# A TensorE-bound attention and gated feed-forward kernel: a new table of lead times, the second batch's query projections at the start, and key projections in pieces of 32 columns

## The chip, the cores and the metric

The kernel runs on 1 core of one Trainium2 chip. The metric is the device time of one execution in microseconds. TensorE's records in a profile are PE (matmuls) and PEld (the weight load that stands ahead of each matmul); DVE is VectorE, ACT is ScalarE, POOL is GpSimd, SP is SyncE, which issues all DMAs here.

## The reference

Four batches, four heads, 1088 positions, 32 values a head. A linear attention is followed by a gated feed-forward with mixing over positions.

```python
# attention, per batch b and head h (r = 8)
phi(x) = outer(S1 @ x, S2 @ x)                  # 64 features a position
kv  = sum_s phi(k)[s] v[s]^T ;  z = sum_s phi(k)[s]
att = phi(q) kv / (phi(q) z + 1e-6)             # -> x [4, 1088, 128]
# feed-forward
h = relu(x @ w_in)                              # [128 -> 1024]
u, v = halves of h                              # 512 each
v_n = (v - mean) / sqrt(var + 1e-6)
v_s = w_spatial @ v_n + b_spatial               # over the 1088 positions
out = (u * v_s) @ w_out                         # [512 -> 128]
```

## The kernel before

**Layout.** Positions are taken in 9 tiles of 128 (`kt`), and, where they are columns, in three pieces `CH` of 424, 332 and 332. Almost all matmuls are float32r in three passes of high and low parts: high times high, high times low, low times high. The bulk is `spatial` (lines 989 and 991 for the high weight, 998 and 1000 for the low one), which for each batch, each of 4 blocks of 128 features (`d`) and each column piece (`c`) adds 9 `kt` into one PSUM bank. `hidden_v` makes the half v of the hidden layer (banks `sd`), its statistics on DVE and its norm; `hidden` makes u (bank `pu`); `gate` multiplies and splits; `out_mm` adds into the banks `po`.

**Batches.** Batch 0's attention (`attention0`) runs first and by itself, with the loads of weights beside it. From then on `main(b)` is written next to `attention(b + 1)`, so that the attention of the next batch runs within the matmuls of this one.

**Two short stretches per attention.** In `keys(b)`, for b = 1 to 3, two blocks of plain float32 matmuls interrupt the float32r ones. The profile shows two passes, each with its weight load, for every float32 matmul that is no transpose. The first stretch, `projections`, projects the three pieces of keys (`project`, line 591) and the first piece of query rows (`query(0, 64)`, line 671). From its banks ACT copies one half (line 596) and DVE builds the key features (line 598). The second stretch, `sums`, adds up kv (`part4`, line 641, 72 matmuls of 33 columns with weights of 32) and projects the other two pieces of query rows. `turned` copies a query projection to SBUF on ACT (tile `abT`, line 658), stores it to DRAM (`abd`, line 772), and `query_features` loads it back spread out (`fa`, `fb`, in the ring `pl` of 6 buffers), to be multiplied on POOL (line 779).

**What sets the order.** Nothing is written in its final order. Each step is given to `op` with its engine, a cost, and what it reads and writes; `schedule` works out a due time for each from the end backwards and then lets each engine take, of the steps that can start about then, the one due first. `LEADS`, a table of some 1,600 numbers (ns), moves the due times of single steps or groups; `Fill` puts small matmuls that nothing reads (line 466) where the plan sees TensorE idle at the start. Engines run the resulting streams in order, and SP's single stream issues every load and store. Where a load's buffer is not free yet, all loads behind it wait.

Of the kernel before, what the change touches and what calls it, by code (L numbers as in the profile page):

```python
# [367 lines left out]
def tile_kernel(ctx: ExitStack, tc: tile.TileContext, kT, qT, vA, sks, idn, msk, wT, w_in, w_out, bsp, out):  # L368
# [218 lines left out]
    def project(ab, xt, at=0):  # L587

        for t in range(3):
            for j in range(2):  # L590
                nc.tensor.matmul(ab_view(ab, at)[64 * j:64 * j + 64, :, t], xt[:, t * P + 64 * j:t * P + 64 * j + 64], sk[:, :NSK], start=True, stop=True)
# [19 lines left out]
    def keys(b, qts=()):  # L611

        xts, vs = [], []
        for g in range(3):
            xt = tl("kt", f"kt{b}{g}", [P, 384])
            load(xt, lambda xt=xt, g=g: xt.ap, kT[b, g], 192, after=AFTER[b])
            v_sb = tl("v", f"v{b}{g}", [P, 3, H * (D + 1)])
            load(v_sb, lambda v_sb=v_sb: v_sb.ap.rearrange("p t c -> p (t c)"), vA[b, g], 198, after=AFTER[b])
            xts.append(xt)
            vs.append(v_sb)  # L620
        kv = bank("sd" if b else "pu", f"kv{b}")

        def part(g, f):
            o = kv[:, :132].rearrange("p (r c) -> p r c", r=2)
            for t in range(3):
                for pr in range(2):
                    for i in range(2):
                        c = 128 * pr + 64 * i
                        nc.tensor.matmul(
                            o[64 * i:64 * i + 64, pr], f[:, t, c:c + 64], vs[g][:, t, 66 * pr:66 * pr + 66],  # L630
                            start=(g == 0 and t == 0 and pr == 0), stop=(g == 2 and t == 2 and pr == 1),
                        )

        def part4(g, f):

            o = kv[:, :68].rearrange("p (r c) -> p r c", r=2)
            for t in range(3):
                for pr in range(2):
                    for j in range(4):
                        c, vc = 128 * pr + 32 * j, 33 * (2 * pr + j // 2)  # L640
                        nc.tensor.matmul(
                            o[32 * j:32 * j + 32, pr, :33], f[:, t, c:c + 32], vs[g][:, t, vc:vc + 33],
                            start=(g == 0 and t == 0 and pr == 0), stop=(g == 2 and t == 2 and pr == 1),
                        )

        if not b:
            for g in range(3):
                f = phi(b, g, xts[g], "k")
                op("PE", 705, f4=True, fn=lambda g=g, f=f: part(g, f), r=[f, vs[g]], w=[kv])
            return kv  # L650

        abTs = []

        def turned(g, ab, o):
            k.part = "q", f"q{b}", f"q{b}.{g}"
            n = TW[g] // 2
            abT = tl("abT", f"abT{b}{g}", [P, 192])
            op("ACT", c_act(n, True), lambda: nc.scalar.copy(out=abT[:, :n], in_=ab[:, o:o + n]), r=[ab], w=[abT])
            abTs.append(abT)
            query_features(b, g, abT, query_fs[-1])  # L660

        abs_ = [bank("sd", f"kab{b}{n}") for n in range(2)]
        at = [(abs_[0], 0), (abs_[0], 192), (abs_[1], 0)]
        qat = [(abs_[1], 192), (kv, 68), (kv, 260)]

        def query(g, m):

            (ab, o), n = qat[g], TW[g] // 2
            for f in range(2):
                for r in range(0, 64, m):  # L670
                    nc.tensor.matmul(ab[64 * f + r:64 * f + r + m, o:o + n], sk[:, r:r + m], qts[g][:, f * n:(f + 1) * n], start=True, stop=True)

        def projections():
            for xt, (ab, o) in zip(xts, at):
                project(ab, xt, o)
            query(0, 64)

        op("PE", 1478, f4=True, fn=projections, r=[*xts, qts[0], (sk, "x")], w=abs_)
        turned(0, *qat[0])
        k.part = "k", f"k{b}"  # L680
        fs = [features(b, g, at[g][0], "k", at[g][1], abTs[:1] if g == 2 else ()) for g in range(3)]

        def sums():
            for g in range(3):
                part4(g, fs[g])
            for g in range(1, 3):
                query(g, 32)

        op("PE", 2070, f4=True, fn=sums, r=[*fs, *vs, *qts[1:], (sk, "x")], w=[kv])
        for g in range(1, 3):  # L690
            turned(g, *qat[g])
        k.part = "k", f"k{b}"
        kvs = tl("ka", f"kvs{b}", [P, 68])
        op("ACT", c_act(68, True), lambda: nc.scalar.copy(out=kvs.ap, in_=kv[:, :68]), r=[kv], w=[kvs])
        return kvs
# [4 lines left out]
    def attention0(st):  # L700

        b = 0
        k.part = "k0", "k0.0"
        kv = keys(b)
        op("DVE", 290, lambda: nc.vector.tensor_tensor(
            out=kd0.ap.rearrange("p r a c -> p (r a) c"), in0=kv[:, :132].rearrange("p (q c) -> p q c", q=4),
            in1=mask[:, 2:].unsqueeze(2).broadcast_to([P, 4, D + 1]), op=ALU.mult,
        ), r=[kv, mask], w=[kd0])
        x_tiles(b, st)
        xh, xl = st["xh"], st["xl"]  # L710
        qts = []
        for g in range(3):
            xt = tl("c", f"qt{b}{g}", [P, 384])
            load(xt, lambda xt=xt, g=g: xt.ap, qT[b, g], 192)
            qts.append(xt)
        k.part = ("q0",)
        qps = [phi(b, g, qts[g], "q") for g in range(3)]
        for g in range(3):
            k.part = "n0", f"n0.{g}"
            tags = ("po", "sp")  # L720
            qp = qps[g]
            qpT = []
            for pr in range(2):
# [36 lines left out]
            op("ACT", c_act(384, True), lambda gs=gs, xp=xp: nc.scalar.copy(out=xh[:, gs], in_=xp[:, :384]), r=[xp], w=[(xh, g)])  # L760
            op("DVE", c_dve(384), lambda gs=gs, xp=xp: nc.vector.tensor_tensor(out=xl[:, gs], in0=xp[:, :384], in1=xh[:, gs].bitcast(F32), op=ALU.subtract), r=[xp, (xh, g)], w=[(xl, g)])
        st["lows"] = [tl("vl", f"vl{b}{d}", [P, NK, P], F32R) for d in range(ND)]
        for g in range(3):
            k.part = "h0", f"h0.{g}"
            hidden_v(b, st, g)
# [391 lines left out]
```

## Time and profile before

| | |
|---|---|
| median of 3 runs | 330.2 us (330.13 to 330.75) |
| profiled execution | 330.07 us, of which the span of its instructions 328.2 us |
| PE busy | 319.7 us, 97% of the span, 2553 matmuls |
| DVE, ACT, POOL busy | 200.8, 151.9, 49.0 us |
| granted TensorE clock | 0.999 over the span |
| DMA | 23.95 MB, 73 GB/s mean, most of it in the first 130 us |

The span runs from the first to the last instruction; the other 1.87 us lie around it. PE is busy in nearly every slice of the page, so time is gained here by less work for TensorE or by fewer of its pauses, and an idle stretch of another engine costs nothing unless TensorE waits for it. Starts of neighbouring matmuls tell its pace better than their durations, which overlap.

### The profile page before, as it was taken

The page shows a single profiled execution, that of the slowest core. Times are in us where ns is not written, and L with a number is a line of the kernel's source. Part 1 is how long each engine was busy: PE and PEld are TensorE (multiplying, and loading weights), DVE is VectorE, ACT ScalarE, POOL GpSimd, SP SyncE. Part 2 cuts the span into 40 slices and gives each one's busy share as a digit, 9 for nine tenths or more (in the row PEclk, how much of TensorE's full clock was granted, in tenths as well). Part 3 has the DMA queues.
Part 4 walks back from the last instruction along what each step waited for, and adds up shares of the span by engine and source line. Part 5 has one row for each costly group of instructions (what it writes and reads, how often), then busy time and mean ns, then how long its engine had stood idle before and what let it go on. Part 6 is the DMA issues. An engine that isn't in the chain of part 4 may idle for free.

```text
span 328.2 us, 6446 instructions
## 1 busy us (share of the span) xinstructions
PE 319.7 (97%) x2553; PEld 305.0 (93%) x2553; DVE 200.8 (61%) x437; ACT 151.9 (46%) x358; POOL 49.0 (15%) x60
## 2 busy tenths in 40 slices
PE   8998999999999899999999999999999999999996
PEld 8987999998999789999999999999999999999995
DVE  4999996457899961468799666379863232231113
ACT  2578947434575452435753554456452142121212
POOL 1000104541610014412000143320000000000000
PEclk9999999999999999999999999999999999999999
DMA  6831369534111245200010334000000010000001
GB/s 214 310 94 50 116 172 312 175 108 147 48 47 44 86 147 177 71 0 7 19 45 15 97 111 138 20 2 0 2 0 1 2 47 23 0 0 2 0 2 68
DMA packets 18960, 23.95 MB, mean 73 GB/s; under 512 B 2546, under 2 KB 18674, under 8 KB 18930
## 3 DMA queue, kind: packets, MB, share of 16 engines
q1 hardware_dynamic: 18930, 23.54, 22.7%
q8 instruction: 20, 0.33, 0.4%
q14 instruction: 10, 0.08, 0.1%
HBM read 20.46 MB, written 3.06 MB: 72 GB/s over the span
## 4 chain that ended last, share of the span: by engine, by line
PE 75%; DVE 9%; DMA 7%; ACT 6%; issue 2%; SPq 0%; ACTq 0%; DVEq 0%
PE sp L989 17%; PE sp L991 15%; PE sp L998 15%; PE sd L439 3%; DMA pl<-in_wT 3%; PE sd L441 3%; PE sd L440 3%; PE pu L439 2%; PE po L440 2%; PE po L439 2%; PE po L441 2%; PE pu L441 2%; PE pu L440 2%; DMA out<-u 2%; PE sp L1000 2%
## 5 line engine op out<-in xcount | busy, mean ns | idle before, releaser
L989 PE MATMUL sp<-wT,vh 128*128 128x332 f32 (+1 forms) x414 | 134.1, 325 | 0.2 <-DVE u L1025 0.2
L991 PE MATMUL sp<-wT,vl 128*128 128x332 f32 (+1 forms) x368 | 118.8, 323 | 0.0
L998 PE MATMUL sp<-wT,vh 128*128 128x332 f32 (+1 forms) x368 | 116.9, 322 | 0.0
L989 PEld LDWEIGHTS sp<-wT,vh 128*128 128x128 f32 x414 | 77.9, 188 | 2.3 <-DVE u L1025 0.8
L991 PEld LDWEIGHTS sp<-wT,vl 128*128 128x128 f32 x368 | 69.2, 188 | 0.3
L998 PEld LDWEIGHTS sp<-wT,vh 128*128 128x128 f32 x368 | 69.1, 188 | 0.1
L1025 DVE TENSOR_TENSOR u<-sp,u 128x332 f32<-128x332 f32 (+1 forms) x40 | 20.5, 516 | 57.4 <-PE sp L1000 41.9
L449 DVE TENSOR_TENSOR g<-u,g 128x332 fp32r<-128x332 f32 (+1 forms) x38 | 23.6, 620 | 17.1 <-PE po L440 10.6
L981 ACT ACTIVATE u<-pu 128x332 f32<-128x332 f32 (+1 forms) x40 | 18.5, 463 | 33.4 <-PE pu L441 22.6
L518 ACT CAST g<-u 128x332 fp32r<-128x332 f32 (+1 forms) x38 | 18.2, 484 | 23.8 <-DVE u L1025 18.2
L843 ACT ACTIVATE vt<-sd 128x512 f32<-128x512 f32 x36 | 21.3, 600 | 15.2 <-PE sd L441 14.4
L845 DVE BATCH_NORM_STATS2 st<-vt 128x6 f32<-128x512 f32 x36 | 24.3, 688 | 5.3 <-ACT vt L843 5.1
L779 POOL TENSOR_TENSOR pl<-pl,pl 128x384 f32<-128x384 f32 (+1 forms) x18 | 18.0, 1005 | 63.6 <-DMA pl<-abd 44.6
L905 ACT CAST vh<-vt 128x384 fp32r<-128x384 f32 x36 | 17.7, 511 | 21.1 <-DVE vt L865 12.4
L823 DVE RECIPROCAL c<-c 128x384 f32<-128x384 f32 (+1 forms) x9 | 21.8, 2417 | 5.1 <-ACT c L821 5.1
L452 POOL TENSOR_TENSOR r<-pl,r 128x384 fp32r<-128x384 f32 (+1 forms) x18 | 18.6, 1037 | 23.5 <-ACT r L518 23.5
L907 DVE TENSOR_TENSOR vl<-vt,vh 128x384 fp32r<-128x384 f32 (+1 forms) x36 | 17.5, 503 | 1.9 <-ACT vh L905 1.7
L439 PE MATMUL pu<-x,wih 128*128 128x332 f32 (+1 forms) x48 | 16.6, 346 | 1.1 <-ACT u L981 0.7
L865 DVE TENSOR_SCALAR vt<-vt,mv,sm 128x512 f32<-128x512 f32 x32 | 16.3, 552 | 0.0
L563 ACT CAST wT<-pl 128x332 fp32r<-128x332 f32 (+1 forms) x27 | 12.9, 496 | 6.8 <-DMA pl<-in_wT 6.6
L441 PE MATMUL pu<-x,wil 128*128 128x332 f32 (+1 forms) x48 | 15.7, 327 | 0.0
L440 PE MATMUL pu<-x,wih 128*128 128x332 f32 (+1 forms) x48 | 15.7, 326 | 0.0
(151 smaller groups left out, 494.1 us busy)
## 6 DMA issues: line engine op xcount, KB each, us to landing
pl<-in_wT SPq DMA_DIRECT2D x18, 166.0 KB
v<-in_vA SPq DMA_DIRECT2D x12, 198.0 KB
kt<-in_kT SPq DMA_DIRECT2D x12, 192.0 KB
pl<-abd SPq DMA_DIRECT2D x12, 192.0 KB
pl<-abd SPq DMA_DIRECT2D x24, 96.0 KB
pl<-in_wT SPq DMA_DIRECT2D x9, 212.0 KB
c<-in_qT SPq DMA_DIRECT2D x9, 192.0 KB
out<-u SPq DMA_DIRECT2D x6, 166.0 KB
```

The source lines that it names most:

```text
L439: nc.tensor.matmul(o, ah, bh, start=start, stop=False)
L440: nc.tensor.matmul(o, ah, bl, start=False, stop=False)
L441: nc.tensor.matmul(o, al, bh, start=False, stop=stop)
L449: return lambda: nc.vector.tensor_tensor(out=o(), in0=a(), in1=bb(), op=ALU.subtract)
L452: return lambda: nc.gpsimd.tensor_tensor(out=o(), in0=a(), in1=bb(), op=ALU.subtract)
L823: op("DVE", 135 + 6.3 * n, lambda x32=x32, n=n: nc.vector.reciprocal(out=x32[:, :n], in_=x32[:, :n]), w=[x32])
L843: op("ACT", c_act(512, True) + 16, lambda pv=pv, t=t: nc.scalar.activation(vt[:, t], pv.ap, AF.Relu), r=[pv], w=[(vt, t)])
L845: op("DVE", 690, lambda stats=stats, t=t: nc.vector.bn_stats(out=stats.ap, in_=vt[:, t]), r=[(vt, t)], w=[stats])
L989: nc.tensor.matmul(sp[:, :cw], vh[:, kt], wTh[:, kt, cs], start=(kt == 0), stop=False)
L991: nc.tensor.matmul(sp[:, :cw], vl[:, kt], wTh[:, kt, cs], start=False, stop=False)
L998: nc.tensor.matmul(sp[:, :cw], vh[:, kt], wTl[:, kt, cs], start=False, stop=False)
L1025: op("DVE", c_dve(cw), lambda: nc.vector.tensor_tensor(out=u.ap, in0=sp[:, :cw], in1=u.ap, op=ALU.mult), r=[sp], w=[u], lead=LEAD[1])
```

## The change

The numbers of `LEADS` are replaced (1,577 entries; most differ). They were found with a plan that also counts TensorE's instructions in blocks of 256; the count itself is not in the kernel, whose `schedule` is as before. Batch 1's query rows are loaded into the `u` ring, projected, copied and stored to DRAM within `attention0` (`early_queries`), ahead of `hidden_v`; their spread-out loads (`expanded`) stay in batch 1's attention. `project` takes its pieces from a parameter: 32 columns in the stretches of batches 1 to 3 (twice the matmuls, as many columns each), 64 in batch 0 as before; batches 2 and 3 also take the first query piece in 32s.

```diff
-LEADS = {'W0': -13000, 'W0.1': 20000, 'W0.3': -5740, ...
+LEADS = {'W0': -5650, 'W0.0': 9780, 'W0.1': -16100, ...
...
-    def project(ab, xt, at=0):
+    def project(ab, xt, at=0, m=64):
         for t in range(3):
-            for j in range(2):
-                nc.tensor.matmul(ab_view(ab, at)[64 * j:64 * j + 64, :, t], xt[:, t * P + 64 * j:t * P + 64 * j + 64], sk[:, :NSK], start=True, stop=True)
+            for j in range(0, P, m):
+                nc.tensor.matmul(ab_view(ab, at)[j:j + m, :, t], xt[:, t * P + j:t * P + j + m], sk[:, :NSK], start=True, stop=True)
...
+        late = b > 1
+        behind = []
         def projections():
             for xt, (ab, o) in zip(xts, at):
-                project(ab, xt, o)
-            query(0, 64)
-        op("PE", 1478, f4=True, fn=projections, r=[*xts, qts[0], (sk, "x")], w=abs_)
-        turned(0, *qat[0])
+                project(ab, xt, o, 32)
+            if late:
+                query(abs_[1], 192, qts[0], 0, 32)
+        op("PE", 1380 if late else 1055, f4=True, fn=projections, r=[*xts, *qts[:late], (sk, "x")], w=abs_)
+        if late:
+            behind = [turned(b, 0, abs_[1], 192)]
+            expanded(b, 0)
...
+        qat = [(kv, 68), (kv, 260)] if late else []
         def sums():
             for g in range(3):
                 part4(g, fs[g])
-            for g in range(1, 3):
-                query(g, 32)
+            for g, (ab, o) in enumerate(qat, 1):
+                query(ab, o, qts[g], g, 32)
-        op("PE", 2070, f4=True, fn=sums, r=[*fs, *vs, *qts[1:], (sk, "x")], w=[kv])
+        op("PE", 2062 if late else 1565, f4=True, fn=sums, r=[*fs, *vs, *qts[1:], (sk, "x")], w=[kv])
...
+    def early_queries():
+        b = 1
+        qts = []
+        for g in range(3):
+            k.part = "q", f"q{b}", f"q{b}.{g}"
+            xt = tl("u", f"qt{b}{g}", [P, 384])
+            load(xt, lambda xt=xt, g=g: xt[:, :TW[g]], qT[b, g, :, :TW[g]], 192)
+            qts.append(xt)
+        for gs in ((0, 1), (2,)):
+            ab = bank("po", f"qab{b}{gs[0]}")
+            op("PE", 326 * len(gs), f4=True, fn=lambda gs=gs, ab=ab: [query(ab, 192 * (g % 2), qts[g], g, 64) for g in gs], r=[*(qts[g] for g in gs), (sk, "x")], w=[ab])
+            for g in gs:
+                turned(b, g, ab, 192 * (g % 2))
...
     def attention(b, st):
+        if b == 1:
+            for g in range(3):
+                expanded(b, g)
+        else:
...
             xt = tl("c", f"qt{b}{g}", [P, 384])
             load(xt, lambda xt=xt, g=g: xt[:, :TW[g]], qT[b, g, :, :TW[g]], 192, after=AFTER[b])
```

Three places show how the streams move. Lines 989, 991, 998 and 1000 are 1011, 1013, 1020 and 1022 in the changed kernel, 671 is 764, 742 is 731, 756 is 745, 658 is 770.

**The start.** TensorE's stream about the first `hidden_v` matmuls of batch 0 (`sd` is their bank, `wih` and `wil` the weights, `sp<-abT,c` transposes of x), before:

```order
L441 MATMUL sd_91<-wih_276,x 128x512
L439 MATMUL sd_129<-wih_276,x 128x512
L440 MATMUL sd_129<-wil_288,x 128x512
L441 MATMUL sd_129<-wih_276,x 128x512
L756 MATMUL sp_301<-abT_125,c_160 128x128 x3
```

and now (`u` holds the early query rows, `po` takes their projection):

```order
L441 MATMUL sd_91<-wih_280,x 128x512
L764 MATMUL po_148<-u_188,sk 64x192 x2
L764 MATMUL po_148<-u_197,sk 64x192 x2
L745 MATMUL sp_308<-abT_121,c_163 128x128 x3
L439 MATMUL sd_126<-wih_280,x 128x512
L440 MATMUL sd_126<-wil_290,x 128x512
L441 MATMUL sd_126<-wih_280,x 128x512
```

Two of the three early pieces now stand there, the third further on, right ahead of the batch's last three hidden blocks and the first `spatial` matmul; 17 fills stand in the stream where 16 did. SP's stream at the same place of the program (`kt<-in_w_in` is the last large load of weights ahead of `wT`, the spatial weight), before:

```order
L446 DMA c_160<-in_qT 128x384
L446 DMA kt<-in_w_in 128x1024
L446 DMA b_64<-in_bsp 83x16
L446 DMA pl_187<-in_wT 128x424
L446 DMA pl_196<-in_wT 128x424
```

and now:

```order
L446 DMA c_163<-in_qT 128x384
L446 DMA kt<-in_w_in 128x1024
L446 DMA u_188<-in_qT 128x384
L446 DMA u_197<-in_qT 128x384
L446 DMA pl_213<-in_wT 128x424
L446 DMA b_64<-in_bsp 83x16
L446 DMA pl_229<-in_wT 128x424
```

Two query loads stand ahead of the first six loads of `wT`; the third stands behind them.

**Batch 1's second stretch.** TensorE's stream where `sums` lies (`kp` the key features, `sd` the bank of kv), before:

```order
L998 MATMUL sp_263<-wT,vh 128x332
L641 MATMUL sd_91<-v,kp_143 32x33 x24
L641 MATMUL sd_91<-v,kp_163 32x33 x24
L641 MATMUL sd_91<-v,kp_148 32x33 x24
L671 MATMUL sd_91<-c_146,sk 32x192 x4
L671 MATMUL sd_91<-c_160,sk 32x160 x4
L989 MATMUL sp_263<-wT,vh 128x332
```

and now:

```order
L1020 MATMUL sp_268<-wT,vh 128x332
L641 MATMUL sd_91<-v,kp_161 32x33 x24
L641 MATMUL sd_91<-v,kp_141 32x33 x24
L641 MATMUL sd_91<-v,kp_144 32x33 x24
L1011 MATMUL sp_268<-wT,vh 128x332
L1022 MATMUL sp_268<-wT,v_93 128x332
```

The query rows are gone from it; batches 2 and 3 keep theirs.

**Between batch 2's two stretches.** TensorE's stream behind the first query piece, before (18 matmuls of 424 columns into `sp` follow the three of `pu`, and then `sums`):

```order
L591 MATMUL sd_91<-sk,kt 64x2x32 x12
L591 MATMUL sd_129<-sk,kt 64x2x32 x6
L671 MATMUL sd_129<-c_160,sk 64x192 x2
L439 MATMUL pu_173<-x,wih_67 128x424
L440 MATMUL pu_173<-x,wih_67 128x424
L441 MATMUL pu_173<-x,wil_71 128x424
L989 MATMUL sp_301<-wT,vh 128x424
```

and now (18 of 332 columns follow the three of `po`, and then `sums`):

```order
L591 MATMUL sd_91<-sk,kt 32x2x32 x24
L591 MATMUL sd_126<-sk,kt 32x2x32 x12
L764 MATMUL sd_126<-c_163,sk 32x192 x4
L439 MATMUL po_148<-g,woh 128x332
L440 MATMUL po_148<-g,woh 128x332
L441 MATMUL po_148<-g,wol 128x332
L1011 MATMUL sp_268<-wT,vh 128x332
```

The 21 matmuls in between are narrower. In batch 3, 72 matmuls of 332 columns lay in between, and 24 do now. ACT's stream there in batch 2, before:

```order
L518 CAST g<-u_735 128x332
L658 COPY abT_125<-sd_129 128x192
L596 COPY ka_63<-sd_91 128x96
L596 COPY ka_69<-sd_91 128x96
L596 COPY ka_63<-sd_129 128x96
```

and now:

```order
L871 ACTIVATE sm_516<-mv_486,eps 128x3
L596 COPY ka_63<-sd_91 128x96
L596 COPY ka_69<-sd_91 128x96
L770 COPY abT_121<-sd_126 128x192
L596 COPY ka_63<-sd_126 128x96
```

The copies for two of the three key features stand ahead of the query's there; in batch 3 they stand behind it, as before.

More of the change, by code (lines that the diff above doesn't have):

```diff
@@ L650, in keys @@
             return kv
[L652 to L660, printed above, removed]
         abs_ = [bank("sd", f"kab{b}{n}") for n in range(2)]
         at = [(abs_[0], 0), (abs_[0], 192), (abs_[1], 0)]
[L664 to L671, printed above, removed]
+        late = b > 1
+        behind = []
         def projections():
             for xt, (ab, o) in zip(xts, at):
-                project(ab, xt, o)
-            query(0, 64)
-        op("PE", 1478, f4=True, fn=projections, r=[*xts, qts[0], (sk, "x")], w=abs_)
-        turned(0, *qat[0])
+                project(ab, xt, o, 32)
[5 more added lines that the diff above has]
+            expanded(b, 0)
         k.part = "k", f"k{b}"
-        fs = [features(b, g, at[g][0], "k", at[g][1], abTs[:1] if g == 2 else ()) for g in range(3)]
+        fs = [features(b, g, at[g][0], "k", at[g][1], behind if g == 2 else ()) for g in range(3)]
+        qat = [(kv, 68), (kv, 260)] if late else []
         def sums():
@@ L685, in sums @@
                 part4(g, fs[g])
-            for g in range(1, 3):
-                query(g, 32)
-        op("PE", 2070, f4=True, fn=sums, r=[*fs, *vs, *qts[1:], (sk, "x")], w=[kv])
-        for g in range(1, 3):
-            turned(g, *qat[g])
+            for g, (ab, o) in enumerate(qat, 1):
+                query(ab, o, qts[g], g, 32)
+        op("PE", 2062 if late else 1565, f4=True, fn=sums, r=[*fs, *vs, *qts[1:], (sk, "x")], w=[kv])
+        for g, (ab, o) in enumerate(qat, 1):
+            turned(b, g, ab, o)
+            expanded(b, g)
         k.part = "k", f"k{b}"
@@ L761, in attention0 @@
             op("DVE", c_dve(384), lambda gs=gs, xp=xp: nc.vector.tensor_tensor(out=xl[:, gs], in0=xp[:, :384], in1=xh[:, gs].bitcast(F32), op=ALU.subtract), r=[xp, (xh, g)], w=[(xl, g)])
+        early_queries()
         st["lows"] = [tl("vl", f"vl{b}{d}", [P, NK, P], F32R) for d in range(ND)]
@@ L765, in attention0, with query, turned, expanded @@
             hidden_v(b, st, g)
-    query_fs = []
-    def query_features(b, g, abT, fs):
+    abds, query_fs = {}, {}
+    def query(ab, o, xt, g, m):
+        n = TW[g] // 2
+        for f in range(2):
+            for r in range(0, 64, m):
+                nc.tensor.matmul(ab[64 * f + r:64 * f + r + m, o:o + n], sk[:, r:r + m], xt[:, f * n:(f + 1) * n], start=True, stop=True)
+    def turned(b, g, ab, o):
+        k.part = "q", f"q{b}", f"q{b}.{g}"
         n = TW[g]
-        abd = tl(None, f"abd{b}{g}", [64, n])
+        abT = tl("abT", f"abT{b}{g}", [P, 192])
+        op("ACT", c_act(n // 2, True), lambda: nc.scalar.copy(out=abT[:, :n // 2], in_=ab[:, o:o + n // 2]), r=[ab], w=[abT])
+        abd = abds[b, g] = tl(None, f"abd{b}{g}", [64, n])
         op("SP", 560, lambda: nc.sync.dma_start(out=abd[:, :].rearrange("r (f c) -> f r c", f=2), in_=abT[:, :n // 2]), r=[abT], w=[abd], kb=n // 4, lag=HBM_LAG[0])
+        return abT
+    def expanded(b, g):
+        k.part = "q", f"q{b}", f"q{b}.{g}"
+        n, abd = TW[g], abds[b, g]
         for pr in range(2):
@@ L779, in query_features @@
             op("POOL", c_pool(n), lambda fa=fa, fb=fb: nc.gpsimd.tensor_tensor(out=fa[:, :n], in0=fa[:, :n], in1=fb[:, :n], op=ALU.mult), r=[fb], w=[fa])
-            fs[g, pr] = fa
+            query_fs[b, g, pr] = fa
+    def early_queries():
+        b = 1
+        qts = []
+        for g in range(3):
+            k.part = "q", f"q{b}", f"q{b}.{g}"
+            xt = tl("u", f"qt{b}{g}", [P, 384])
[6 more added lines that the diff above has]
+                turned(b, g, ab, 192 * (g % 2))
     def attention(b, st):
@@ L786, in attention @@
         qts = []
-        for g in range(3):
-            k.part = "q", f"q{b}", f"q{b}.{g}"
-            xt = tl("c", f"qt{b}{g}", [P, 384])
-            load(xt, lambda xt=xt, g=g: xt[:, :TW[g]], qT[b, g, :, :TW[g]], 192, after=AFTER[b])
-            qts.append(xt)
+        if b == 1:
+            for g in range(3):
+                expanded(b, g)
+        else:
+            for g in range(3):
+                k.part = "q", f"q{b}", f"q{b}.{g}"
+                xt = tl("c", f"qt{b}{g}", [P, 384])
+                load(xt, lambda xt=xt, g=g: xt[:, :TW[g]], qT[b, g, :, :TW[g]], 192, after=AFTER[b])
+                qts.append(xt)
         k.part = "k", f"k{b}"
-        fs = {}
-        query_fs.append(fs)
         kv = keys(b, qts)
@@ L814, in attention @@
             for pr in range(2):
-                f = fs[g, pr]
+                f = query_fs[b, g, pr]
                 fh, fl = tl("r", f"fh{b}{g}{pr}", [P, 384], F32R), tl("r", f"fl{b}{g}{pr}", [P, 384], F32R)
```

2 lines of the change are left out of this document (1 added, 1 removed).

## The prediction

> **What bounds the kernel now.** I read the page's sums first, then TensorE's waits, then the windows, and at last its timeline about each place that the change touches.
>
> ```profile
> PE 319.7 (97%) x2553; PEld 305.0 (93%) x2553; DVE 200.8 (61%) x437; ACT 151.9 (46%) x358; POOL 49.0 (15%) x60
> ...
> q8 instruction: 20, 0.33, 0.4%
> ...
> PE sd L671 <- issue: 1.5, 1, 1.5
> ...
> PE sd L439 <- ACT vt L843: 0.9, 1, 0.9
> PE pu L439 <- ACT u L981: 0.7, 2, 0.4
> ...
> 0.00:32.20 32.20, 29.67 (x294) 26.48 (x295) 26.50 (x72) 20.01 (x46) 1.21 (x8) 1.00 0.52 165
> ...
> 60.00:120.00 60.00, 57.79 (x677) 53.88 (x676) 45.63 (x96) 32.25 (x83) 17.23 (x19) 1.00 0.30 92
> 120.00:180.00 60.00, 59.72 (x383) 57.08 (x382) 38.60 (x80) 28.20 (x65) 12.29 (x14) 1.00 0.17 53
> 180.00:240.00 60.00, 59.71 (x499) 56.70 (x498) 41.97 (x89) 30.70 (x73) 13.09 (x14) 1.00 0.16 51
> 240.00:300.00 60.00, 60.00 (x368) 59.38 (x368) 17.69 (x38) 16.57 (x39) 0.00 (x0) 1.00 0.03 10
> ```
>
> TensorE is the bound: from 32 us on it sits idle for 2.21 us in the window to 120, 0.28 in that to 180, 0.29 in that to 240. The largest piece is 1.5 us, its releaser "issue", which means that nothing the profile shows held it. So three things can move the time: that pause, the work that TensorE does after 32 us, and its other waits, 2.78 - 1.5 = 1.3 us in these windows.
>
> **The pause in batch 2's second stretch.** The timeline of PE at the second stretch of batches 1, 2 and 3, with the counts of matmuls up to their starts and up to the pause:
>
> ```profile
> 67.69 1.52 PE L641 MATMUL sd<-v,kp 128*32 128x33 f32 x142
> ...
> 69.05 0.80 PE L671 MATMUL sd<-c,sk 128*32 128x192 f32 x15
> 69.77 0.42 PE L989 MATMUL sp<-wT,vh 128*128 128x332 f32 x1
> ...
> 112.40 1.51 PE L641 MATMUL sd<-v,kp 128*32 128x33 f32 x143
> ...
> 115.54 0.80 PE L671 MATMUL sd<-c,sk 128*32 128x192 f32 x15 [1.50 <-issue]
> 116.27 0.42 PE L439 MATMUL po<-g,woh 128*128 128x332 f32 x1
> ...
> 185.52 1.48 PE L641 MATMUL sd<-v,kp 128*32 128x33 f32 x143
> ...
> 187.55 0.42 PE L439 MATMUL po<-g,woh 128*128 128x332 f32 x1
> ...
> 0.00:67.68 67.68, 64.70 (x521) 1.00 0.56 178
> 0.00:112.39 112.39, 109.14 (x966) 1.00 0.45 139
> 0.00:113.90 113.90, 110.65 (x1111) 1.00 0.44 138
> 0.00:185.50 185.50, 180.48 (x1568) 1.00 0.35 111
> ```
>
> The same stretch takes 69.77 - 67.69 = 2.08 us in batch 1, 3.87 in batch 2, 2.03 in batch 3: the pause costs 1.8. Why there? The page has 20 packets of instructions with 0.33 MB, 16.5 KB each, against 2 x 2553 = 5106 instructions: one packet is some 256. With two instructions a matmul, the stretches start at instructions 1042, 1932 and 3136, which is 18, 140 and 64 past a multiple of 256, and are 320 long. The pause comes at 2222, 174 past one. Every one of the three crosses a place 174 past a multiple of 256, but only batch 2's crosses two of them, at its 34th and its 290th instruction. So I take it that TensorE may run into a block while the next is fetched, and that it stops where it uses up 256 instructions before that fetch ends: from the first crossing (a tenth of the stretch's 1.5 us, about 112.55) to the restart at 115.54 are 3.0 us. A stretch hits that only where it starts 110 to 174 past a multiple. I counted the same for the changed streams (two for a matmul, four for a float32 one, two for a transpose): its second stretches start 86, 30 and 60 past one, with 288, 320 and 320 instructions. The second crossing lies 56, 80 and 50 instructions behind their ends, so 25 and more ordinary matmuls at about 0.15 us, 3.7 us, are still to come. The first stretches, with 144 or 160 instructions now, cross one place at most. The pause goes: -1.7 us, between -1.8 and 0. I stay 0.1 short of all of it since the restart behind any stretch costs something.
>
> [...]
>
> **Batch 1's queries.** They leave two stretches. Of the first piece, the timeline shows batch 2's, of the same form:
>
> ```profile
> 106.75 1.27 PE L591 MATMUL sd<-sk,kt 128*64 128x64 f32 x36
> 107.85 0.50 PE L671 MATMUL sd<-c,sk 128*64 128x192 f32 x4
> 108.27 0.46 PE L439 MATMUL pu<-x,wih 128*128 128x424 f32 x1
> ```
>
> From start to start it takes 108.27 - 107.85 = 0.42 us; the other two in batch 1 take 69.77 - 69.05 = 0.72, of which I leave 0.1 for the step back to wide matmuls. So 1.0 us of work leaves the part where TensorE never rests. It lands in the start, where there is room:
>
> ```profile
> 25.12 0.35 PE L441 MATMUL pu<-x,wil 128*128 128x424 f32 x1
> 26.39 0.50 PE L439 MATMUL sd<-wih,x 128*128 128x512 f32 x1 [0.92 <-ACT vt L843]
> ...
> 28.09 0.55 PE L466 MATMUL po<-z 128*128 128x64 f32 x4
> 28.87 0.46 PE L439 MATMUL pu<-x,wih 128*128 128x424 f32 x1 [0.22 <-ACT kp L981]
> ```
>
> Between 25.12 and 28.87 an idle stretch (1.27 from start to start, where about 0.2 is usual) and fills with a wait (0.78) give 1.85 us of cover for 1.0 of work. Without it the whole 1.0 comes back. ACT gets three copies there, 0.32 us each by the row quoted below (0.96), and loses them in batch 1; SP gets three loads and three stores earlier, POOL nothing. The changed order also has two u copies less ahead of the first high part of v, so I charge only a fill's 0.1: -1.0 + 0.1 = -0.9, between -1.0 and 0.
>
> **Pieces of 32 columns.** Three stretches with 72 pairs of records instead of 36. If a pair costs what line 641's do (1.51 / 143 = 10.6 ns), 72 take 0.76 us, against the 1.10 from 106.75 to 107.85; if it costs what line 591's do, they take 2.2. Line 671 decides: 8 records in pieces of 32 over 192 columns and 8 over 160 take 0.72 us, 0.36 for eight, and 4 in pieces of 64 took 0.42. Halving a piece left the time as it was or a little lower. I take -0.07 for each stretch, -0.2 in all, between -1.0 and +0.2. The other end, an unchanged cost for each record (+3.3), is excluded by line 671, where it fell from 0.42 / 4 = 105 ns to 45.
>
> **Waits for key features.** In batches 2 and 3 less work lies between the stretches. The chain in batch 2 before:
>
> ```profile
> 108.39 0.32 ACT L658 COPY abT<-sd 128x192 f32<-128x192 f32 x1
> 108.61 0.39 ACT L596 COPY ka<-sd 128x96 f32<-128x96 f32 x2
> ...
> 109.18 2.68 DVE L598 TENSOR_TENSOR kp<-ka,sd 128x768 f32<-128x768 f32 x3
> ```
>
> The features end at 111.86, 3.6 us behind the first stretch's end at 108.27, and the second stretch came at 112.40, 4.1 behind it. Now 21 matmuls of 332 columns, about 0.15 us each, give 3.1 us in batch 2, and 24 give 3.6 in batch 3. With the chain as it was TensorE would wait 0.5 and 0 us. In batch 2 ACT now copies the key half first, which saves up to 0.32. I charge 0.25, between 0 and 0.8.
>
> **The other waits** (1.3 us) fall elsewhere in a new order. Nothing in the rows says which way; I take 0, between -0.9 and +1.2.
>
> **The sum.** -1.7 - 0.9 - 0.2 + 0.25 = -2.55, from the profiled execution's 330.07 to 327.5; the median shown, 330.2, is 0.13 above that, so 327.6. I say 327.5.
>
> **Rivals.**
> 1. *The pause stays*, as it isn't a fetch or strikes at another crossing. For: one event is a thin basis, and the changed stream has 5326 instructions by the same count, a block more. Against: batches 1 and 3. Time: 327.5 + 1.7 = 329.2. [...]
> 2. *The start pays for the queries.* Two loads of 0.2 MB now stand ahead of the first `wT`:
>
> ```profile
> GB/s 214 310 94 50 116 172 312 175 108 147 48 47 44 86 147 177 71 0 7 19 45 15 97 111 138 20 2 0 2 0 1 2 47 23 0 0 2 0 2 68
> ...
> 14.46 0.54 ACT L563 CAST wT<-pl 128x424 fp32r<-128x424 f32 x1
> ...
> 44.57 0.47 ACT L563 CAST wT<-pl 128x332 fp32r<-128x332 f32 x1 [2.72 <-DMA pl<-in_wT]
> ...
> ACT wT L563 <- DMA pl<-in_wT: 6.6, 4, 2.7
> ```
>
> At the second slice's 310 GB/s, 0.39 MB take 1.3 us, and ACT's casts of `wT` stand ahead of the copies that the query features of batch 0 wait for. Against: ACT waited for these loads four times in all, and the first of the four stands at 44.57; the cast at 14.46 followed ACT's work at once. If the loads (1.3, and 0.5 for the third), the copies (0.96) and TensorE's 1.0 all came on the path, 3.8 us against the 3.05 gained: 330.8, slower. It decides from the point where the first `spatial` matmul, at 32.2 us before, starts later than 32.2 + 3.0. With half of it the result is 329.4.
> 3. *The new order waits less*, at the place where batch 1's query loads no longer crowd the others: 1.3 us of waits shrink to 0.4, pieces gain 0.6: 326.2.
>
> **How the numbers follow.** A measurement here can tell 0.2% from no change, 0.66 us: faster is below 329.5, slower above 330.9. My forecast with its smaller variants (326.3 to 328.7) has 0.62, rival 3 0.13, rival 1 0.10, rival 2 by half 0.07 and in full 0.08. Faster: 0.62 + 0.13 + 0.05 of rival 1 + 0.02 of rival 2 = 0.82. Within 0.2%: 0.10; slower: 0.08. The range reaches from rival 3 with a little to spare, 325.8, to rivals 1 and 2 by half, 329.6.
>
> **What would show it.** Right: no "issue" wait of PE in line 641 or 764, and batch 2's second stretch at about 2.1 us; batch 1's at about 1.5; first `spatial` matmul at 32 to 33 us; 72 records of line 591 in about 1.0 us; PE's waits ahead of line 641 below 0.5 us. Wrong: an "issue" wait in any stretch, line 591 at 2 us, a first `spatial` matmul past 34, or new waits of several tenths each on ACT's u or DVE's gate in the 30 to 240 us window.

## The result: 0.7% faster, 328.17 us against 330.35

Five runs of each on one chip: the changed kernel has a median of 328.17 us (327.66 to 329.01), the kernel before 330.35 (330.13 to 331.32); the ratio is 0.9932 with a 95% interval from 0.991 to 0.9955. The profiled execution took 328.65 us, against 330.07 of the one before: 1.4 us less, where the medians differ by 2.2. First the sums of the page after:

```profile
PE 319.2 (98%) x2663; PEld 304.8 (93%) x2663; DVE 194.3 (59%) x437; ACT 152.3 (47%) x358; POOL 49.6 (15%) x60
q8 instruction: 21, 0.34, 0.5%
```

One packet of instructions more than before, 21 against 20, at 220 more instructions of TensorE (5326 against 5106, a matmul and a weight load for each record). The windows, to be read against those of before:

```profile
0.00:32.20 32.20, 29.67 (x302) 25.81 (x303) 25.64 (x70) 19.70 (x46) 1.21 (x8) 1.00 0.60 186
32.20:60.00 27.80, 27.42 (x215) 26.36 (x214) 23.93 (x53) 19.11 (x44) 2.24 (x3) 1.00 0.55 165
60.00:120.00 60.00, 59.28 (x711) 55.18 (x710) 45.61 (x101) 33.51 (x84) 21.32 (x22) 1.00 0.35 106
120.00:180.00 60.00, 59.51 (x574) 56.92 (x573) 40.12 (x90) 30.34 (x73) 13.57 (x15) 1.00 0.24 71
180.00:240.00 60.00, 59.73 (x351) 57.46 (x350) 36.85 (x80) 29.24 (x66) 11.25 (x14) 1.00 0.09 28
```

TensorE's idle time from 60 to 120 us fell from 2.21 to 0.72 us, by the 1.5 us of the pause; that from 32.2 to 60 us rose from nothing to 0.38, and that from 120 to 240 us from 0.57 to 0.76. The list of PE's waits has no "issue" any more; of the rest:

```profile
PE sd L440 <- POOL r L452: 0.5, 1, 0.5
PE sd L439 <- ACT vt L865: 0.5, 1, 0.5
PE sp L1013 <- DVE vl L958: 0.4, 1, 0.4
```

The three second stretches and batch 1's first one (start, busy time, shape, count):

```profile
52.82 1.21 PE L591 MATMUL sd<-sk,kt 128*32 128x64 f32 x72
53.97 0.46 PE L1020 MATMUL sp<-wT,vh 128*128 128x424 f32 x1
...
66.68 2.03 PE L641 MATMUL sd<-v,kp 128*32 128x33 f32 x144
68.64 0.42 PE L1011 MATMUL sp<-wT,vh 128*128 128x332 f32 x1
...
113.41 1.51 PE L641 MATMUL sd<-v,kp 128*32 128x33 f32 x143
...
115.47 0.42 PE L439 MATMUL po<-g,woh 128*128 128x332 f32 x1
...
167.01 1.51 PE L641 MATMUL sd<-v,kp 128*32 128x33 f32 x143
...
169.09 0.42 PE L1011 MATMUL sp<-wT,vh 128*128 128x332 f32 x1
```

Batch 2's second stretch takes 115.47 - 113.41 = 2.06 us instead of 3.87, batch 3's 2.08. Batch 1's takes 1.96, though 16 of its records are gone: only 0.12 less than before. Its first stretch takes 1.15 instead of 1.53.

Now the sum over the profiled executions, by the starts of the matmuls: the six stretches together went from 12.57 to 10.18 us (-2.39). Against that stands the start: the first `spatial` matmul came at 32.95 instead of 32.23 us, and three matmuls of 424 columns that used to stand ahead of it (0.57 us) stand behind it now, so the start cost 1.29. The two executions differ by 1.42, so -0.32 is left for everything else behind the first `spatial` matmul. That is a remainder and no wait that can be pointed at, since the idle time listed there, apart from the pause, rose.

### The profile page after: what moved, and what is told of

It reads as the page before. It is cut to its first block, busy times and chain, and to the rows that moved or that the text cites. A ratio compares the mean times of both kernels' runs of the same rounds, so it can differ in the third digit from the quotient of the medians.

```text
span 326.8 us, 6680 instructions
## 1 busy us (share of the span) xinstructions
PE 319.2 (98%) x2663; PEld 304.8 (93%) x2663; DVE 194.3 (59%) x437; ACT 152.3 (47%) x358; POOL 49.6 (15%) x60
## 4 chain that ended last, share of the span: by engine, by line
PE 72%; DMA 10%; ACT 5%; DVE 4%; POOL 3%; SPq 2%; issue 2%; POOLq 0%; ACTq 0%
PE sp L1011 16%; PE sp L1020 15%; PE sp L1013 15%; DMA pl<-abd 4%; DMA pl<-in_wT 4%; PE sd L440 3%; PE sd L439 2%; PE sd L441 2%; PE po L439 2%; PE po L441 2%; PE po L440 2%; PE pu L439 2%; DMA v<-in_vA 2%; PE sp L1022 2%; PE pu L441 2%
## 5 line engine op out<-in xcount | busy, mean ns | idle before, releaser
L1003 ACT ACTIVATE u<-pu 128x332 f32<-128x332 f32 (+1 forms) x40 | 18.5, 462 | 30.4 <-PE pu L441 27.7
L449 DVE TENSOR_TENSOR g<-u,g 128x332 fp32r<-128x332 f32 (+1 forms) x38 | 20.3, 533 | 15.7 <-PE po L440 9.9
L518 ACT CAST r<-pl 128x384 fp32r<-128x384 f32 (+1 forms) x18 | 8.8, 493 | 18.7 <-POOL pl L784 15.3
L598 DVE TENSOR_TENSOR kp<-ka,sd 128x768 f32<-128x768 f32 x15 | 13.7, 948 | 6.0 <-DMA out<-kp 3.6
L439 PE MATMUL pu<-x,wih 128*128 128x332 f32 (+1 forms) x48 | 16.4, 341 | 0.3 <-ACT u L1003 0.2
```

What stands on the lines that cost most here:

```text
L439: nc.tensor.matmul(o, ah, bh, start=start, stop=False)
L449: return lambda: nc.vector.tensor_tensor(out=o(), in0=a(), in1=bb(), op=ALU.subtract)
L518: op("ACT", c_act(n), lambda: nc.scalar.copy(out=hi(), in_=x()), r=r, w=wh)
```

## The experiments

Four questions: is the pause a matter of TensorE's instruction count, what did the start cost, what was the pause worth, and why does batch 1's second stretch gain so little?

### Does the pause follow the instruction count?

Three edits of the kernel before shift the count ahead of the stretches and nothing else in the order. Each fill becomes two small matmuls (64 instructions more), three (128 more), or none (64 less; nothing reads the fills):

```diff
-        nc.tensor.matmul(homes[tag, slot][:, :64], z9.ap, z9[:, :64], start=True, stop=True)
+        for _ in range(2):
+            nc.tensor.matmul(homes[tag, slot][:, :8], z9.ap, z9[:, :8], start=True, stop=True)
```

> The kernel before, with each of its 16 fills at the start written as two matmuls of 8 columns: 64 more TensorE instructions ahead of everything else, the same order. Theory 1 (a pause where 256 instructions are used up before the fetch that began at the last crossing ends): the second stretches now start 82, 204 and 128 past a multiple of 256, so the pause leaves batch 2 and comes in batch 3, about 1.5 us, behind some 300 instructions of its second stretch, among the query matmuls. Theory 2 (the pause belongs to batch 2's stretch, by a wait that the profile doesn't show): it stays in batch 2 at 1.8 us, and batch 3 keeps 2.03 us.

> The same with three matmuls for each fill: 128 more instructions. Theory 1: the second stretches start 146, 12 and 192 past a multiple; the pause comes in batch 1, 1.6 us or so behind some 284 instructions, none in batch 2, at most 0.3 us in batch 3. Theory 2: it stays in batch 2.

> The kernel before without its 16 fills: 64 instructions less. Theory 1: starts at 210, 76 and 0; no pause anywhere, and all three second stretches take 2.0 to 2.1 us, so the time falls by 1.8 us, less what the start loses or gains without fills (-1 to +1): 328.4, between 327.4 and 329.4. Theory 2: the pause stays and the time is 329.2 to 331.2.

The fourth is the changed kernel with its old pieces of 64 columns in the first stretches, its order kept; the count falls by 72 ahead of batch 1's second stretch and by 152 ahead of batch 2's:

```diff
-                project(ab, xt, o, 32)
+                project(ab, xt, o, 64)
...
-                query(abs_[1], 192, qts[0], 0, 32)
+                query(abs_[1], 192, qts[0], 0, 64)
```

> The changed kernel with the first stretches in pieces of 64 columns again, the order as it is. By the rows of line 591 and of the query piece behind it the pieces themselves are worth 0.06 us a stretch, 0.2 us in all. Theory 1: 72 to 80 instructions fewer in each first stretch move the second ones to 14, 134 and 84 past a multiple; batch 2's crosses at 40 and 296, and the pause of about 1.5 us is back there: 328.2 + 0.2 + 1.5 = 329.9. Theory 2: no pause, 328.4.

The timeline of PE with two small fills for each, in batch 3's second stretch (lines stand one further on):

```profile
191.47 1.48 PE L642 MATMUL sd<-v,kp 128*32 128x33 f32 x143
...
192.78 0.51 PE L672 MATMUL sd<-c,sk 128*32 128x192 f32 x5
194.95 0.78 PE L672 MATMUL sd<-c,sk 128*32 128x192 f32 x10 [1.66 <-issue]
```

With three, in batch 1's:

```profile
85.56 1.53 PE L642 MATMUL sd<-v,kp 128*32 128x33 f32 x143
...
87.87 0.80 PE L672 MATMUL sd<-c,sk 128*32 128x192 f32 x15 [0.65 <-issue]
```

And in the changed kernel with pieces of 64, in batch 2's:

```profile
111.97 1.53 PE L641 MATMUL sd<-v,kp 128*32 128x33 f32 x143
...
113.33 0.49 PE L764 MATMUL sd<-c,sk 128*32 128x192 f32 x3
114.86 0.79 PE L764 MATMUL sd<-c,sk 128*32 128x192 f32 x12 [1.04 <-issue]
```

The pause went to batch 3, to batch 1, and back to batch 2, each time to the one stretch whose start the count puts between 110 and 174 past a multiple of 256 (128, 146, 134), and without fills, where none is (210, 76, 0), all three stretches took 2.03 to 2.08 us. It struck after 150, 145 and 148 records, that is at 428, 436 and 430 instructions with the start added: 172, 180 and 174 past a multiple, where the trace before had 174. From the first crossing to the restart it took 3.3, 2.2 and 2.7 us (3.0 before); the stretch lost 2.2, 1.0 and 1.5.

The fetches themselves are among the profile's DMA packets, on the queue q8: packets of 16,384 bytes, one for about every 256 of TensorE's instructions (20 for 5106 in the page before, 21 for 5326 in the page after). Here is the one that belongs to each of the four pauses (before, two small fills, three, pieces of 64), each in the window of 0.1 us that holds its start; the last number is the packet's time as a share of 16 DMA engines in that window, so that 59.9% stands for 0.96 us:

```profile
q8 instruction: 1, 0.02, 59.9%
q8 instruction: 1, 0.02, 72.0%
q8 instruction: 1, 0.02, 63.6%
q8 instruction: 1, 0.02, 79.7%
```

They start at 113.17, 192.50, 85.41 and 112.17 us, and TensorE restarts 1.3 to 1.4 us after each has landed; in the kernel before the next one starts at 117.15 us, behind the restart at 115.54. So these four pauses end behind the landing of one block of instructions, as theory 1 has it, and their size is not a constant. It was larger the later that packet started: the stretch lost 1.0 us where it started 0.3 us ahead of the first crossing, 1.5 at the crossing, 1.8 and 2.2 where it started 0.6 and 0.8 us behind it. Beside the other 19 packets of before, and beside all 21 of after, the list of PE's waits has no "issue".

The times missed what was expected. The small fills made the start long (first `spatial` matmul at 37.85 and 48.99 us; 337.74 and 349.94 us, one execution each). Without fills it came at 34.35, and the kernel at 332.68 (ratio 1.006, 1.003 to 1.009), where 328.4 was expected. The version with 64 columns came at 327.88 (ratio 0.992, 0.9888 to 0.9952), no slower than the changed kernel although its pause was back; 329.9 was expected, so its trace speaks for theory 1 and its time does not. That and the run without fills, slower although its pause was gone, made me ask what the pause was worth.

### What was the pause worth?

The kernel before with pieces of 32 in its first stretches as its only edit moves the second stretches to 98, 44 and 48:

```diff
-                project(ab, xt, o)
-            query(0, 64)
+                project(ab, xt, o, 32)
+            query(0, 32)
```

> The kernel before with pieces of 32 columns in the first stretches (keys and first query piece) as its only edit: order, loads and queries stay. Theory 1 (TensorE pauses where it uses up 256 instructions faster than the next block arrives): by the count the second stretches now start 98, 44 and 48 past a multiple of 256 instead of 18, 140 and 64. Batch 2's crosses one place only, so its 1.8 us go: stretches of 2.1, 2.1 and 2.0 us, no wait named issue inside a stretch. Batch 1's crosses its first place at instruction 76 of 320, 0.5 us in, and the second lies only 12 instructions behind its end, some 2.5 us after the first where the traces before needed 3.0: a rest of 0 to 0.5 us may stand a few matmuls behind batch 1's stretch, at about 70 us. First stretches 1.47 us instead of 1.53. Time: 330.2 - 1.8 - 0.2 + 0.2 = 328.4, between 328.0 and 328.8. Theory 2 (the pause belongs to batch 2's place in the program or to the order around it): batch 2's stretch stays at 3.9 us, time 330.0.

329.83 us, ratio 0.9997 (0.9976 to 1.0017), where 328.4 was expected: no change. The pause was gone (2.08, 2.06 and 2.03 us in the three stretches). Whether a rest of it stood behind batch 1's can't be told: one step at 70.7 us is 0.45 us too long, but is put down to DVE, and before has 0.23 there. But its waits, and the end of the wait in the timeline:

```profile
PE pu L439 <- ACT u L981: 2.2, 2, 1.5
```

```profile
112.25 1.51 PE L641 MATMUL sd<-v,kp 128*32 128x33 f32 x143
...
125.62 0.35 PE L441 MATMUL po<-g,wol 128*128 128x424 f32 x1
127.52 0.47 PE L439 MATMUL pu<-x,wih 128*128 128x424 f32 x1 [1.55 <-ACT u L981]
...
172.43 0.26 PE L591 MATMUL sd<-sk,kt 128*32 128x64 f32 x4
```

In the kernel before the same matmul waited too, but shorter, as TensorE came there 1.9 us later:

```profile
127.54 0.35 PE L441 MATMUL po<-g,wol 128*128 128x424 f32 x1
128.17 0.46 PE L439 MATMUL pu<-x,wih 128*128 128x424 f32 x1 [0.28 <-ACT u L981]
```

The excess over the usual step grew from 0.44 to 1.71 us. From batch 2's second stretch to batch 3's first it is 173.13 - 112.40 = 60.73 us before and 172.43 - 112.25 = 60.18 without the pause: of 1.81 us, 1.3 were given back 12 us later. What ends the wait is on ACT and SP:

```profile
121.17 0.41 SPq L967 DMA_DIRECT2D out<-u  x1
```

```profile
125.99 0.51 ACT L518 CAST r<-pl 128x384 fp32r<-128x384 f32 x1 [4.48 <-POOL pl L779]
127.02 0.45 ACT L981 ACTIVATE u<-pu 128x332 f32<-128x332 f32 x1 [0.52 <-DMA out<-u]
```

ACT's u copy waits for the store that frees its buffer, which SP issued behind three value loads (119.42 us, 1.66 for the three), and stands behind a cast that waits for POOL and its loads. So the next kernel moves those three loads, and nothing else:

```diff
...
     order = k.schedule()
+    late = [o for o in order if getattr(o, "name", "") in ("v30:1", "v31:1", "v32:1")]
+    order = [o for o in order if o not in late]
+    place = 1 + next(n for n, o in enumerate(order) if getattr(o, "name", "") == "fb221:1")
+    order[place:place] = late
...
```

> q_pieces with one move in SP's stream: the three loads of batch 3's values (0.6 MB, needed at about 184 us) stand behind batch 2's last query load instead of ahead of the store out<-u at 121 us. In q_pieces the pause was gone, yet 1.3 of its 1.8 us came back as a wait of 1.5 us ahead of pu at 127 us: ACT's next u copy waited for that store, which landed 5.7 us after its issue at 121.17, and ACT's cast of query features ahead of it waited until 126 for POOL, whose last load ran beside the same three. Theory W (the pause had covered this chain, and the chain hangs on the value loads): the store is issued by 119.5 and has landed before 124, POOL's features come about 1.5 us earlier, the wait at 127 falls below 0.3 us, the way from batch 2's second stretch to batch 3's first takes 58.6 to 59.0 us instead of 60.2, and the time is 329.8 - 1.4 = 328.4, between 328.1 and 328.9. Rival (the features' chain is as long without the loads, since it is the spread-out loads' own time): the wait stays above 1 us, the way at 59.8 or more, time 329.6.

```profile
120.11 0.39 SPq L967 DMA_DIRECT2D out<-u  x1
```

```profile
125.66 0.51 ACT L518 CAST r<-pl 128x384 fp32r<-128x384 f32 x1 [3.40 <-POOL pl L779]
126.08 0.44 ACT L981 ACTIVATE u<-pu 128x332 f32<-128x332 f32 x1
```

With batch 2's stretch at 112.98 and the next first stretch at 171.71, the way takes 58.73 us, and the wait at 127 is gone. 328.92 us, ratio 0.9959 (0.9942 to 0.9977); 328.4 was expected, and at most 328.9. Since all of this kernel came 0.7 us later than the one without the move, the u copy at 126.08 lies 1.7 us earlier against the stretch: 1.1 of it because the cast ahead of it does, and the rest because it no longer waits for the store. (Of the missing 0.5 us the profile shows a wait of 1.5 us at 61 us, for the same kind of u copy, where q_pieces waited 0.7.) Theory W holds: the pause had covered a chain of ACT, SP and loads, which these three loads held up. The store's issue, at 120.11, and the features, 1.1 us earlier, fell a little short of what it forecast, and the move was not run with the pause in place.

In the changed order the chain isn't in the way: three u copies stand ahead of the first cast in ACT's stream there, where two did. ACT in the profile of after:

```profile
124.31 0.44 ACT L1003 ACTIVATE u<-pu 128x332 f32<-128x332 f32 x1
125.39 0.93 ACT L518 CAST r<-pl 128x384 fp32r<-128x384 f32 x2 [0.64 <-POOL pl L784]
```

The way from batch 2's second stretch to batch 3's first, in a second profile of the changed kernel and, second, with the pause put back by pieces of 64:

```profile
112.95 1.51 PE L641 MATMUL sd<-v,kp 128*32 128x33 f32 x143
...
160.64 0.26 PE L591 MATMUL sd<-sk,kt 128*32 128x64 f32 x4
```

```profile
161.17 1.27 PE L591 MATMUL sd<-sk,kt 128*64 128x64 f32 x36
```

That is 160.64 - 112.95 = 47.69 us against 161.17 - 111.97 = 49.20: 1.5 us, all of what the stretch lost. Four kernels of the next sections that have this order and no pause took 47.68 to 47.87 us. The changed kernel's first profile took 48.41, with a wait of 0.7 at 139 us for ACT's `vt`. As a whole the version with 64 columns still wasn't slower: it was at least 0.4 us faster than any of these from the first `spatial` matmul to this stretch, which lies ahead of the pause. One profile can't tell whether that is its own or chance, and so the 1.5 us stand in the profiles but in no measured time.

### What did the start cost?

In the profile of after, ACT's step on the second half of `w_in` is late (before, then after):

```profile
13.78 0.68 ACT L501 ACTIVATE v<-kt 128x512 f32<-128x512 f32 x1
```

```profile
15.59 0.69 ACT L501 ACTIVATE v<-kt 128x512 f32<-128x512 f32 x1 [1.20 <-DMA u<-in_qT]
```

It is late by 1.8 us before any early query matmul runs. Two causes are possible in SP's stream: the early query loads beside it, and the new order of the first 13 loads, in which SP reached this load at 9.68 instead of 8.21 us. So, on one chip with five rounds: the changed kernel again; with the query loads behind the sixth `wT` load; with the first 13 loads in the order of before; and with both.

```diff
...
     order = k.schedule()
+    moved = ['kt00:1', 's_raw:1', 'kt01:1', 'kt02:1', 'mask_sb:1', 'wi_raw1:1', 'v00:1', 'qt00:1', 'v01:1', 'v02:1', 'ident_sb:1', 'qt01:1', 'qt02:1', 'wi_raw0:1', 'wt00:1', 'b32:1', 'wt10:1', 'wt20:1', 'wt30:1', 'wt40:1', 'wt50:1', 'qt10:1', 'qt11:1', 'qt12:1']
+    at = [n for n, o in enumerate(order) if getattr(o, "eng", "") == "SP"][:len(moved)]
+    named = {order[n].name: order[n] for n in at}
+    for n, name in zip(at, moved):
+        order[n] = named[name]
...
```

This is the list with both; the early query loads are `qt10` to `qt12`.

> The changed kernel as it is, beside the three that follow on the same chip: 328.2, between 327.6 and 329.0. Its profile tells whether ACT's abs of the second half of w_in (line 501 at 15.59 in the first profile, 13.78 in the kernel before) and batch 1's second stretch (1.96 us instead of the 1.4 that the missing queries would leave) are late in every execution.

> The changed kernel, with the two early loads of query rows that stand ahead of the first wT load moved behind the sixth, beside the third; every other stream as it was. Theory A (the start is late since these 0.39 MB share the DMA engines with the load of w_in that ACT's line 501 waits for): line 501 comes 0.8 to 1.3 us sooner, the first spatial matmul 0.6 to 1.2 us sooner, the time falls by as much, to 327.2. Theory B (it is late since SP's loads stand in another order, where one waits for a lane of the first w_in load): line 501 gains under 0.3 us and the time stays within 0.3 of the changed kernel's.

> The changed kernel with SP's first 13 loads in the order that the kernel before has (the small mask ahead of w_in, the first keys ahead of sks), the early query loads where they are. Theory A: within 0.3 us of the changed kernel. Theory B: the second w_in load is issued at about 8.3 instead of 9.5 to 9.7 us, line 501 and the first spatial matmul come 0.6 to 1.2 us sooner, and the time falls by as much.

> Both: the first 13 loads as in the kernel before, and the query loads behind the sixth wT load. Line 501 at 13.8 us as in the kernel before by either theory; first spatial matmul at 31.6 to 32.0 us, time 326.9 to 327.4, below the changed kernel's by 0.8 to 1.3. If the queries' TensorE and ACT work (1.0 us each) is what makes the start late, and not the loads, the time stays at 328.

| | median | ratio to before, interval | first `spatial` matmul in the profile |
|---|---|---|---|
| changed kernel again | 328.16 us | 0.9937, 0.9918 to 0.9956 | 32.05 us |
| query loads late | 327.35 | 0.9909, 0.9896 to 0.9922 | 32.17 |
| first loads as before | 327.46 | 0.9930, 0.9904 to 0.9955 | 31.37 |
| both | 326.72 | 0.9904, 0.9887 to 0.9922 | 32.20 |

The medians say 0.8 us for the one, 0.7 for the other, 1.4 for both; the ratios, which go by means, say 0.9, 0.2 and 1.1. The intervals of the first and last row overlap by a little, those of the others by much, so there is a gain of about 1 us for both, and how it divides between the two theories is not shown.

Nor do the profiles settle it: the same changed kernel had its first `spatial` matmul at 32.95 in one execution and at 32.05 in another, and the ACT step above at 15.59 and 14.67. The start varies by 0.9 us between executions, as much as was sought. "Both" was expected to have that step at 13.8; it came at 14.78, while the kernel of the last section, with the same loads there, had it at 13.72. Over all profiles with fills of 64 columns the step came at 13.10 to 13.78 in the order of before (three executions), at 14.63 to 15.59 with the first loads in the new order (four), and at 13.71 to 14.78 with the first loads put back (four). So the changed kernel's start is late by more than one execution's chance, and the first loads probably have a part in it. Not all of an earlier start arrives, either: of the 0.9 us between the two executions of the changed kernel 0.5 were left at batch 2's second stretch (113.41 and 112.95), as waits in between took up the rest. "Both" is the fastest kernel of the study, 3.5 us below before.

### Why did batch 1's second stretch gain only 0.1 us?

Its 144 records of line 641 took 1.83 us from the first start to the last where the other batches' took 1.33, with three steps of 75 to 193 ns between weight loads, on no semaphore. In the profiles of the changed order up to then some 190 to 220 GB/s of loads ran there, and in all other stretches under 70. So the kernel with both edits, with most of that traffic taken out:

```diff
+        m = 16 if b == 1 else n
...
-            op("SP", 610, lambda fa=fa, pr=pr: nc.sync.dma_start(out=fa[:, :n], in_=abd[16 * pr:16 * pr + 16].unsqueeze(1).broadcast_to([16, R, n])), r=[abd], w=[fa], kb=n // 2, lag=HBM_LAG[1])
+            op("SP", 610, lambda fa=fa, pr=pr, m=m: nc.sync.dma_start(out=fa[:, :m], in_=abd[16 * pr:16 * pr + 16, :m].unsqueeze(1).broadcast_to([16, R, m])), r=[abd], w=[fa], kb=n // 2, lag=HBM_LAG[1])
...
```

The loads of `fb` are cut in the same way.

> e_both with the spread-out loads of batch 1's query projections cut to 16 of their 384 columns (the rest of those columns is left out of the computation). Question: why batch 1's second stretch takes 1.7 to 2.0 us where 144 matmul passes at the pace of the other batches take 1.4. Theory T (DMA traffic in the stretch delays TensorE: 184 to 220 GB/s ran there, 0 to 56 in every stretch without gaps): the rate falls below 60 GB/s, the gaps of 70 to 200 ns go, the stretch takes 1.40 to 1.50. Theory P (the POOL cast of wT, the DVE multiply or the place in the instruction stream): all three stay as they are, and so does the stretch, 1.65 to 2.0. The time says little of it: 0.3 less by the stretch, and up to 1.1 less since the query features come earlier for the matmul that waits for them at 72 us.

The windows over most of line 641 in the changed kernel and, second, here (the last number is GB/s):

```profile
66.68:68.48 1.80, 1.80 (x144) 1.64 (x143) 0.87 (x2) 0.00 (x0) 0.93 (x2) 1.00 0.56 193
```

```profile
65.82:67.61 1.79, 1.79 (x144) 1.70 (x143) 0.76 (x2) 0.00 (x0) 1.79 (x3) 1.00 0.14 18
```

The traffic fell to a tenth, and the 1.8 us stayed: theory T is wrong. Across runs of the changed order the stretch took 1.68 to 1.99, with one to three gaps, at about the 62nd, 102nd and 141st record whatever its place in the count (14 or 86 past a multiple). SP issues three or four loads back to back beside it in all of these, and at most two in the others. Each of the larger gaps begins 0.1 to 0.3 us behind the start of such an issue (in the profile of after at 67.73 and 68.28 us, with issues at 67.53 and 68.16), but in batch 3's stretch a single one, at 167.79 us, left none. What causes the gaps is open. The time, 326.35, says little, as the loads were left out.

### One wait more

In the version with both, TensorE still waited 1.1 us at 72 us for POOL's query features. Its first two pairs of attention matmuls were put 11 matmuls later:

```diff
...
+    for o in order[here:there + 1]:
+        if getattr(o, "name", "") in ("nd100:1", "nd101:1") or isinstance(o, Op) and any(id(d) in seen for d in o.deps):
+            later.append(o)
...
```

> e_both with one more move in TensorE's stream: batch 1's first two pairs of attention matmuls (sd<-r, the first of which waits 1.1 us at 72 us for POOL's query features) stand 11 matmuls later, behind work that is ready. If that wait is only a matter of order: it goes and nothing takes its place, 326.7 - 1.0 = 325.7, between 325.3 and 326.1. Rival: what hangs on these two (ACT, DVE, the next pair) is late instead and TensorE waits as long a little further on: 326.5 to 326.9.

```profile
59.14 0.46 PE L439 MATMUL po<-x,woh 128*128 128x424 f32 x1 [0.38 <-ACT x L518]
...
78.82 0.42 PE L440 MATMUL po<-g,woh 128*128 128x332 f32 x1 [0.76 <-DVE g L449]
```

The wait at 72 went, and one of 0.9 us at 78 came for DVE's gate, which is the rival. Another 1.1 us at 58 to 60 lies ahead of the edit: this execution's start was 1.05 us earlier, at 31.15, and the waits there gave it back. 327.31 us, ratio 0.9916 (0.9893 to 0.9939): no gain over 326.72, and above what either theory forecast.

## Why the prediction was right, step by step

The median of 328.17 is 0.7 us above the forecast of 327.5 and inside the range. The terms came out less well than the sum, and that the sum came so near is partly luck.

- **The pause, -1.7.** Right for the stretch, and for the reason given: it fell by 1.81 us, the pause moved at will with the count, and each pause ended 1.3 to 1.4 us behind the landing of a block of instructions. Rival 1 fell. As a gain in time the term is not confirmed: with the pause put back the kernel came at 327.88 us, where this term would have it near 329.9, and its interval ends at 0.9952, 0.7 us above the changed kernel's ratio. What the step lacked is the question what comes next behind the pause. In the order of before the answer was a wait that took 1.3 of it back; that the changed order had no such wait was not worked out.
- **Batch 1's queries, -0.9.** The step that failed. The first stretch gave 0.38, near the 0.42. The second gave 0.12 and not 0.62, by the gaps in line 641. And "I charge only a fill's 0.1" was wrong: the start cost 1.29 us in the profiled execution and 0.39 in the other (0.18 earlier, 0.57 of matmuls moved behind), and by the medians 1.4 us come back when SP's loads are put right. How that divides between rival 2's query loads and the new order of SP's first loads, a term that the prediction did not have at all, is not shown. ACT's copies and TensorE's work had no part in it, as their cover held: from ACT's step on `w_in` to the first `spatial` matmul it took 17.4 us against 18.5 before, of which 0.6 are the three matmuls that moved.
- **Pieces of 32, -0.07 a stretch.** Right: 1.53 to 1.47 us in batches 2 and 3. Batch 1's 72 records took 1.15, the other two's 1.03.
- **Waits for key features, +0.25.** None came; batch 2's stretch began 0.24 us behind the matmul ahead of it (0.28 before).
- **The other waits, 0.** As remainders, -0.3 in the first profile and -0.4 in the second. The wait at 127 us is gone, others at 35, 73 and, in the first alone, 139 are new.

The changed kernel's second profile, with the earlier start, ends 2.5 us below before, which is the forecast's sum, but by other terms: the queries gave some 0.7 less than forecast, and the pause (0.1), the waits that didn't come (0.25) and the remainder (0.4) made up for it. One number in the rivals was wrong: the 3.05 us that rival 2 sets against its cost counts the 0.25 of waits as a gain. By the sum's own terms it is 2.55, and rival 2 in full would have been 331.3 and not 330.8; nothing hung on it.

## What to carry to other kernels

Where a bound engine pauses, look up what waits for whom some 10 us behind it before pricing the pause: another chain may take most of the gain back, as it did here (1.3 of 1.8 us) until three loads were moved. Count the instructions ahead of a run of very short ones. Here two in 9 ns (144 records in 1.33 us) use up 256 in about 1.2 us, an estimate from that pace, while 2.2 to 3.3 us went by from the first crossing to the restart. The count, which any edit upstream shifts, told in the seven kernels compared here whether and in which batch a pause came, and the instruction packets among the profile's DMAs show what it ended behind. And for work moved "into idle time at the start", look at the loads that it brings and at what else the new order does to those that the start waits for, not only at the idle time.

## What was not expected of the hardware

- Without the fills the granted clock was lower in seven of ten executions: 0.983 to 0.994 over the span, and 1.000 in the other three, against 0.998 to 1.000 in the 13 of before beside them. In the profiled one the window from 8 to 16 us shows a granted clock of 0.57 with TensorE busy for 7.09 us of 8, where before has 1.00 and 8.00, and the first `spatial` matmul came 2.1 us later:

```profile
8.00:16.00 8.00, 7.09 (x115) 6.74 (x116) 5.85 (x10) 1.98 (x5) 0.00 (x0) 0.57 0.97 357
```

- Small fills came out worse here than none: two of 8 columns instead of one of 64 made the start 5.6 us longer, three 16.8, none 2.1. The granted clock was 0.63 from 8 to 16 us with two and 0.64 from 32 to 40 us with three (0.990 and 0.985 over the span), and 8 us at 0.64 lose 2.9 by that share, which is a part of it; the rest is open.
- The way from the first crossing of a place 174 past a multiple of 256 to the restart isn't fixed: 2.2 to 3.3 us in four pauses. That from the landing of the block to the restart nearly is: 1.3 to 1.4 us.
